# Attention and gated feed-forward on one core: the ordering's TensorE durations set to the trace, and 90 idle products for 160

## The chip, the core and the metric

The kernel runs on one core of a Trainium2 chip. TensorE multiplies matrices, VectorE (DVE), ScalarE (ACT) and GpSimd (POOL) work on elements, SyncE (SP) issues the DMAs. The metric is the device time of one execution in microseconds; the time of a kernel is the median of its runs. A profiled execution has its own time, and the span from its first to its last instruction lies inside it.

## The reference

```python
# q, k, v: (4, 8, 768, 64) f32; n_sink = 4, window = 128
scores = q @ k.T / 8
keep = (pos_k < n_sink) | ((0 <= rel) & (rel < window))     # rel = pos_q - pos_k
a = softmax(where(keep, scores, -1e9)); attn = a @ v
x = attn.transpose(0, 2, 1, 3).reshape(3072, 512)
h = x @ w_in                       # (512, 2048), float64
out = (h * cos(h)) @ w_out         # (2048, 512), float64, result f32
```

Only a band of 128 keys and the first few (the sinks) are kept for each query, and everything behind it is a feed-forward layer whose two products are most of the work.

## The kernel before

**Tiling.** The 3072 tokens are 12 chunks of 256 (two blocks of 128 queries). A chunk has 8 heads of attention and then 8 *slots* of the feed-forward layer; a slot is 256 of the 2048 inner columns. Products are made in fp32r with each operand split into a high and a low part, so each is three matmuls: high by high, high by low, low by high.

**A head.** The scores `s` (line 739 for the first 24 heads, "early" ones, in plain fp32; line 795 for the others) go into one PSUM tile with one buffer. The mask step (808, VectorE) adds the mask and takes the row's extreme; the next score needs that tile back. Then come the exponential (817, ScalarE), the denominator (826, 827, VectorE), the normalisation (835 on ScalarE or 837 on VectorE or POOL), the transposition `tp` (897, TensorE), a copy or a split of it (368, 370, 906, 913), the product with V, `av` (927 early, 951 later), and the split of the result into `xhi` and `xlo`. An early head makes the low part with a small matmul against minus the identity (325). Early heads also turn q and k on TensorE (715, `qk`).

**A slot.** `h` (379) is 24 matmuls in four steps of six. Then: turns (388, ScalarE), whole and rest (394, 399, VectorE), cosine (404, ScalarE), gate (409, VectorE), the split into `ghi` (415, ScalarE) and `glo` (421, VectorE or POOL), and `acc` (430), 12 matmuls in four steps of three. After the eighth slot the two output blocks are copied (368 or 370) and stored.

**Weights.** They come as float64 in 32 pieces through two raw buffers. VectorE turns each into f32 in three steps (483, 489, 495), ScalarE rounds it to the high part (516), VectorE or POOL makes the low part (519). Later all pieces are read again for a range check (534). This conversion runs beside the attention of the first chunks.

**What sets the order.** Nothing is left to run-time choice but waiting: each engine has one fixed list. `Plan.order` makes the lists at build time. Every step has the engines that could do it, an expected duration on each, its predecessors, the buffers it needs and a due time. The planner walks forward in expected time; when an engine is free it takes the ready step with the earliest due time, and where several engines could do a step, the expected durations decide who takes it. A change of ScalarE's table between exponential and cosine is charged. The expected durations thus set the order on all engines, though no instruction depends on them. `GATE` is when the engines are expected to begin, `PRE` when VectorE and ScalarE may begin the steps marked `ahead` (the weight steps); what starts before `GATE` is written ahead of the program's branch. `SPE` is the expected delay from any other engine's step to TensorE.

**Idle products.** `fill` (line 1174 of the profile) is a 128x128 by 128x256 matmul of the minus identity into a PSUM tile nobody reads. `FILL` of them are given to the planner with due times behind everything else, so TensorE takes one whenever no other step is ready in the planner's time, until they are used up.

Of the kernel before, what the change touches and what calls it, by code (L numbers as in the profile page):

```python
# [28 lines left out]
    "DV": 4.41, "DX": 7.018, "FILL": 160, "GHI": 2, "GLO": 2, "L": 1, "LAG": 4.21, "LEAD": 18.263, "NEH": 24,  # L29
    "NM": 1.373, "NW": 2.093, "NWF": 0.026, "PB": 5, "PEN": 10.744, "PL": 3, "POOLF": 0.675, "POOLPEN": 2.303,  # L30
    "PRE": 4.5, "R": 2, "RAW": 2, "SAME": 0.13, "SEM": 0.2, "SPE": 0.3, "STEP": 5.59, "T": 6.142, "TH": -1.227,
    "WARM": 11, "WI": -18.566, "WO": 7.302, "WS": 1.56, "WS2": -0.177, "WT": 2, "XV": 2,
}
GATE = 5.4
# [138 lines left out]
def attn_moe_kernel(ctx, tc, q, k, v, n_sink, window, w_in, w_out, out):  # L173
# [20 lines left out]
    NEH = int(C["NEH"]) // 2 * 2  # L194
# [106 lines left out]
    env = Rec()  # L301
# [38 lines left out]
    def split_x(plan, x, a, p, t, odd=None):  # L340

        add, buf = plan.add, plan.buf
# [7 lines left out]
        if odd is None:  # L350
            j = add(sub(NT), x_lo(x, a, p, odd), d, t + 0.3, port=True)
        else:
            m = add([("PE", 0.11)], x_minus(x, p, odd), [i], t + 0.3)
            users.append(m)
            env.minus.users.append(m)
            j = add([("ACT", act(NT, False)), ("DVE", dve(NT))], x_lo(x, a, p, odd), d + [m], t + 0.6)
# [188 lines left out]
    def dense(plan, x, a, s, t, T, w_in_ready, w_out_ready, acc_banks, h_bank):  # L545
# [8 lines left out]
        if True:  # L554
# [23 lines left out]
            for tt in range(FG):  # L578
                for j in range(CB):
                    d = [a5, a6] + w_out_ready[s] + (accs[j].users[:1] or [accs[j]])  # L580
                    late = 2.6 * j if a == len(chunks) - 1 and s >= NSLOT - 2 else 0.3 * j
                    i = add([("PE", 0.655)], out_mm(o, x, tt, j), d, t + C["LAG"] * T + (0.0, 1.95)[tt] + late)
# [21 lines left out]
    def banded_path():  # L604
# [383 lines left out]
        def before_softmax(g, o):  # L988
# [111 lines left out]
        def after_softmax(g, o):  # L1100
# [4 lines left out]
            if o.early:  # L1105
# [44 lines left out]
            y0 = add([("PE", 0.5)], values(o), deps, t + C["DA"] + 4.0)  # L1150
# [28 lines left out]
        for n in range(int(C["FILL"])):  # L1179
            idle.users.append(add([("PE", 0.11)], fill(n), idle.users[:1] or [idle, env.minus], 1e4 + n))  # L1180
# [229 lines left out]
```

## Time and profile before

| what | value |
|---|---|
| time, median of 3 runs | 789.77 us (788.59 to 789.86) |
| profiled execution | 790.24 us |
| its span | 788.4 us, granted TensorE clock 0.994 |
| TensorE busy | 762.5 us, 97% |
| VectorE, ScalarE, POOL busy | 641.8, 577.5, 172.0 us |
| HBM read | 64.10 MB |

A line of the groups reads: line, engine, operation, output <- inputs, shapes, count, then busy time and the mean of one in ns, then the engine's idle time before these instructions and what ended it. A matmul's record includes its way through the array, so matmuls overlap; what one costs in a sequence is read from start to start. A line of the timeline begins with start and duration in us. A line of waits reads: who <- for whom, us in total, times, longest.

### The profile page before, as it was taken

The page shows a single profiled execution, that of the slowest core. Times are in us where ns is not written, and L with a number is a line of the kernel's source. Part 1 is how long each engine was busy: PE and PEld are TensorE (multiplying, and loading weights), DVE is VectorE, ACT ScalarE, POOL GpSimd, SP SyncE. Part 2 cuts the span into 40 slices and gives each one's busy share as a digit, 9 for nine tenths or more (in the row PEclk, how much of TensorE's full clock was granted, in tenths as well). Part 3 has the DMA queues.
Part 4 walks back from the last instruction along what each step waited for, and adds up shares of the span by engine and source line. Part 5 has one row for each costly group of instructions (what it writes and reads, how often), then busy time and mean ns, then how long its engine had stood idle before and what let it go on. Part 6 is the DMA issues. An engine that isn't in the chain of part 4 may idle for free.

```text
span 788.4 us, 15691 instructions
## 1 busy us (share of the span) xinstructions
PE 762.5 (97%) x5087; PEld 671.9 (85%) x5087; DVE 641.8 (81%) x1672; ACT 577.5 (73%) x1363; POOL 172.0 (22%) x239
## 2 busy tenths in 40 slices
PE   7999999999999999999999999999999999999996
PEld 6766777788999889898989899999998999999994
DVE  5777889876899879879979999889789979875442
ACT  1666878688787787787887877888898887785332
POOL 1113111000112214232233334322012232420000
PEclk8999999999999999999999999999999999999999
DMA  5554455423275265346455442332142242210000
GB/s 149 152 155 116 140 155 154 110 62 56 42 181 123 47 167 145 79 121 160 104 134 153 109 103 49 55 75 42 34 86 53 47 87 38 42 38 6 27 1 32
DMA packets 215676, 71.53 MB, mean 91 GB/s; under 512 B 204320, under 2 KB 204320, under 8 KB 215584
## 3 DMA queue, kind: packets, MB, share of 16 engines
q1 hardware_dynamic: 215584, 70.43, 37.6%
q8 instruction: 42, 0.69, 0.4%
q14 instruction: 50, 0.41, 0.2%
HBM read 64.10 MB, written 6.29 MB: 89 GB/s over the span
## 4 chain that ended last, share of the span: by engine, by line
PE 73%; DVE 13%; DMA 6%; ACT 3%; SPq 2%; issue 2%; DVEq 0%; POOL 0%; ACTq 0%; POOLq 0%
PE h L379 26%; PE acc L430 25%; PE tp L897 4%; PE av L951 4%; PE s L795 4%; DMA raw<-in_moe_w_out_dram 3%; PE idle L1174 3%; PE s L739 3%; PE av L927 2%; DMA raw<-in_moe_w_in_dram 2%; DVE p L808 1%; SPq L677 1%; DVE wt L534 1%; DVE r L399 1%; DMA xq<-in_q_dram 1%
## 5 line engine op out<-in xcount | busy, mean ns | idle before, releaser
L379 PE MATMUL h<-xhi,whi_in 128*128 128x256 f32 x768 | 224.4, 292 | 2.6 <-DVE r L409 2.6
L379 PE MATMUL h<-xlo,whi_in 128*128 128x256 f32 x768 | 216.4, 282 | 0.0
L379 PE MATMUL h<-xhi,wlo_in 128*128 128x256 f32 x768 | 216.3, 282 | 0.0
L379 PEld LDWEIGHTS h<-xhi,whi_in 128*128 128x128 f32 x768 | 145.2, 189 | 16.3 <-issue 5.2
L430 PE MATMUL acc<-whi_out,ghi 128*128 128x512 f32 x384 | 155.6, 405 | 0.0
L430 PE MATMUL acc<-wlo_out,ghi 128*128 128x512 f32 x384 | 151.4, 394 | 0.0
L379 PEld LDWEIGHTS h<-xhi,wlo_in 128*128 128x128 f32 x768 | 145.5, 189 | 6.8
L430 PE MATMUL acc<-whi_out,glo 128*128 128x512 f32 x384 | 150.6, 392 | 0.0
L379 PEld LDWEIGHTS h<-xlo,whi_in 128*128 128x128 f32 x768 | 145.2, 189 | 0.1
L808 DVE CUSTOM_DVE_ANT_0 p<-s,mk 128x264 f32<-128x264 f32 (+1 forms) x192 | 76.4, 398 | 24.9 <-PE s L795 12.1
L817 ACT ACTIVATE p<-p,st 128x264 f32<-128x264 f32 (+1 forms) x192 | 93.2, 488 | 0.5
L430 PEld LDWEIGHTS acc<-whi_out,glo 128*128 128x128 f32 x384 | 72.2, 188 | 16.6
L404 ACT ACTIVATE r<-r 128x512 f32<-128x512 f32 x96 | 59.7, 631 | 35.6 <-DVE r L399 32.2
L850 POOL TENSOR_TENSOR vr<-v,vr 128x192 fp32r<-128x192 f32 (+1 forms) x63 | 41.1, 652 | 172.4 <-ACT vr L845 127.1
L415 ACT CAST ghi<-r 128x512 fp32r<-128x512 f32 x96 | 59.0, 615 | 24.8 <-PE acc L430 23.0
L430 PEld LDWEIGHTS acc<-whi_out,ghi 128*128 128x128 f32 x384 | 72.5, 189 | 5.1 <-issue 0.5
L430 PEld LDWEIGHTS acc<-wlo_out,ghi 128*128 128x128 f32 x384 | 72.9, 190 | 4.3
L409 DVE TENSOR_TENSOR r<-h,r 128x512 f32<-128x512 f32 x96 | 64.4, 679 | 13.1 <-ACT r L404 12.7
L399 DVE TENSOR_TENSOR r<-yt,r 128x512 f32<-128x512 f32 x96 | 74.0, 770 | 1.0
L421 DVE TENSOR_TENSOR glo<-r,ghi 128x512 fp32r<-128x512 f32 x71 | 49.6, 699 | 29.3 <-ACT ghi L415 28.8
L795 PE MATMUL s<-r,l 128*128 128x264 f32 (+2 forms) x288 | 62.7, 295 | 6.8 <-DVE r L786 3.8
L388 ACT ACTIVATE yt<-h 128x512 f32<-128x512 f32 x96 | 57.0, 593 | 8.3 <-PE h L379 6.5
(128 smaller groups left out, 1471.2 us busy)
## 6 DMA issues: line engine op xcount, KB each, us to landing
raw<-in_moe_w_in_dram SPq DMA_DIRECT2D x32, 512.0 KB, 4.6
raw<-in_moe_w_out_dram SPq DMA_DIRECT2D x32, 512.0 KB, 3.7
xk<-in_k_dram SPq DMA_DIRECT2D x256, 48.0 KB, 2.0
out_dram<-raw SPq DMA_DIRECT2D x24, 256.0 KB, 2.2
v<-in_v_dram SPq DMA_DIRECT2D x64, 96.0 KB, 2.1
xq<-in_q_dram SPq DMA_DIRECT2D x144, 32.0 KB, 1.9
v<-in_v_dram SPq DMA_DIRECT2D x32, 64.0 KB, 2.0
xq<-in_q_dram SPq DMA_DIRECT2D x24, 64.0 KB, 2.5
```

Source lines behind the costliest of these rows:

```text
L379: nc.tensor.matmul(out=o.h[:, t, :], lhsT=w[:, c, fs], rhs=xx[:, c, :], start=(c == 0 and n == 0), stop=(c == NC - 1 and n == 2),)
L388: nc.scalar.activation(out=o.y, in_=o.h, func=AF.Copy, scale=INV2PI, bias=0.25)
L399: e.tensor_tensor(out=o.r, in0=o.y, in1=o.r, op=ALU.subtract)
L404: nc.scalar.activation(out=o.r, in_=o.r, func=AF.Sin, scale=TWOPI_DOWN)
L409: nc.vector.tensor_tensor(out=o.r, in0=o.h, in1=o.r, op=ALU.mult)
L415: nc.scalar.copy(out=o.ghi, in_=o.r)
L421: e.tensor_tensor(out=o.glo, in0=o.r, in1=f32(o.ghi), op=ALU.subtract)
L430: nc.tensor.matmul(out=x.acc[j], lhsT=gg[:, t, j * P : (j + 1) * P], rhs=w[:, f, :], start=(f == 0 and n == 0), stop=(f == NFT - 1 and n = ...
L795: nc.tensor.matmul(out=o.s_ps[j][:, :w], lhsT=o.l[:, j * P : (j + 1) * P], rhs=r.rearrange("p n s -> p (n s)")[:, c0 : c0 + w], start=(n = ...
L808: nc.vector.tensor_tensor_reduce(out=o.p[:, j, :w], in0=o.s_ps[j][:, :w], in1=masks[min(o.i0 + j, 2)][:, :w], op0=ALU.add, op1=ALU.min, sc ...
L817: nc.scalar.activation(out=o.p[:, j, :w], in_=o.p[:, j, :w], func=AF.Exp, bias=o.lead.st[:, 0, o.nth, j : j + 1], scale=-1.0, accum_out=o. ...
L850: e.tensor_tensor(out=o.vr[:, :, 1, :], in0=o.v32, in1=f32(o.vr)[:, :, 0, :], op=ALU.subtract)
```

## The change

The expected durations of TensorE's steps are replaced: a step of `h` 0.714 us instead of 0.655, of `acc` 0.696 instead of 0.655, an early score `w / 650 + 0.235` instead of `w / 600 + 0.02`, other scores 0.245 instead of 0.23, an early `av` 0.15 longer, a later one 0.64 instead of 0.5 where the sinks are in it, the small matmul of line 325 0.3 instead of 0.11, an idle product 0.12 instead of 0.11. `GATE` goes from 5.4 to 9.0, `PRE` from 4.5 to 7.3, `SPE` from 0.3 to 0.2. `FILL` goes from 160 to 90. The arithmetic of the result is untouched; the lists of all five engines come out in another order.

```diff
-    "DV": 4.41, "DX": 7.018, "FILL": 160, "GHI": 2, "GLO": 2, "L": 1, "LAG": 4.21, "LEAD": 18.263, "NEH": 24,
+    "DV": 4.41, "DX": 7.018, "FILL": 90, "GHI": 2, "GLO": 2, "L": 1, "LAG": 4.21, "LEAD": 18.263, "NEH": 24,
-    "PRE": 4.5, "R": 2, "RAW": 2, "SAME": 0.13, "SEM": 0.2, "SPE": 0.3, "STEP": 5.59, "T": 6.142, "TH": -1.227,
+    "PRE": 7.3, "R": 2, "RAW": 2, "SAME": 0.13, "SEM": 0.2, "SPE": 0.2, "STEP": 5.59, "T": 6.142, "TH": -1.227,
-GATE = 5.4
+GATE = 9.0
...
-                        add([("PE", 0.655)], h_mm(o, x, tt, half), d + mm[-1:], t + C["DH"] + (3.5, 5.8)[tt] + 0.6 * half)
+                        add([("PE", 0.714)], h_mm(o, x, tt, half), d + mm[-1:], t + C["DH"] + (3.5, 5.8)[tt] + 0.6 * half)
...
-                    i = add([("PE", 0.655)], out_mm(o, x, tt, j), d, t + C["LAG"] * T + (0.0, 1.95)[tt] + late)
+                    i = add([("PE", 0.696)], out_mm(o, x, tt, j), d, t + C["LAG"] * T + (0.0, 1.95)[tt] + late)
...
-                    dur, fn, deps, used = o.w[j] / 600 + 0.02, scores_pe(o, oe, j), oe.kr, (oe.btq, oe.btk)
+                    dur, fn, deps, used = o.w[j] / 650 + 0.235, scores_pe(o, oe, j), oe.kr, (oe.btq, oe.btk)
...
-            idle.users.append(add([("PE", 0.11)], fill(n), idle.users[:1] or [idle, env.minus], 1e4 + n))
+            idle.users.append(add([("PE", 0.12)], fill(n), idle.users[:1] or [idle, env.minus], 1e4 + n))
```

More of the change, by code (lines that the diff above doesn't have):

```diff
@@ L352, in split_x @@
         else:
-            m = add([("PE", 0.11)], x_minus(x, p, odd), [i], t + 0.3)
+            m = add([("PE", 0.3)], x_minus(x, p, odd), [i], t + 0.3)
             users.append(m)
@@ L1064, in before_softmax @@
                     oe = heads[g - o.odd]
-                    dur, fn, deps, used = o.w[j] / 600 + 0.02, scores_pe(o, oe, j), oe.kr, (oe.btq, oe.btk)
+                    dur, fn, deps, used = o.w[j] / 650 + 0.235, scores_pe(o, oe, j), oe.kr, (oe.btq, oe.btk)
                 else:
-                    dur, fn, deps, used = 0.23, scores(o, j), [o.ql, *o.kr], (o.bl, b1, b2)
+                    dur, fn, deps, used = 0.245, scores(o, j), [o.ql, *o.kr], (o.bl, b1, b2)
                 c0 = add([("PE", dur)], fn, [*deps, bs], t - 5 * T + C["DS"] + (3.25, 5.55)[j])
@@ L1115, in after_softmax @@
                 y0 = add(
-                    [("PE", 0.215 * o.n + 0.05)], values_pe(o, x), [p1, i, x.y0 if o.odd else x.bav], t + C["DA"] + 4.0
+                    [("PE", 0.215 * o.n + 0.2)], values_pe(o, x), [p1, i, x.y0 if o.odd else x.bav], t + C["DA"] + 4.0
                 )
@@ L1149, in after_softmax @@
                 deps += oe.sinks
-            y0 = add([("PE", 0.5)], values(o), deps, t + C["DA"] + 4.0)
+            y0 = add([("PE", 0.64 if o.sj else 0.5)], values(o), deps, t + C["DA"] + 4.0)
             for bb in (bvr, bhi, blo):
```

## The prediction

> **What bounds the kernel now.** I read the engine shares first, then the chain of work that ended last, then TensorE's own row of time by stage.
>
> ```profile
> span 788.4 us, 15691 instructions
> PE 762.5 (97%) x5087; PEld 671.9 (85%) x5087; DVE 641.8 (81%) x1672; ACT 577.5 (73%) x1363; POOL 172.0 (22%) x239
> ...
> by line: PE h L379 26.4%; PE acc L430 24.8%; PE tp L897 4.1%; PE av L951 4.1%; PE s L795 3.6%; DMA raw<-in_moe_w_out_dram 3.1%; PE idle L1174 2.9%; PE s L739 2.6%; issue 2.4%; PE av L927 2.2%; DMA raw<-in_moe_w_in_dram 2.1%; DVE p L808 1.1%
> ```
>
> TensorE sets the time: 97% busy, and the chain runs mostly through it. The entry to look at is `PE idle L1174`: 2.9% of 788.4 is 22.9 us in which the chain passes through products that nobody needs. Where they stand is told by the stretches (PE busy, PEld, DVE, ACT, POOL, granted clock, DMA share, GB/s):
>
> ```profile
> 10.00:20.00 10.00, 10.00 (x55) 8.38 (x53) 7.83 (x25) 1.98 (x4) 0.00 (x0) 0.77 0.53 147
> 20.00:30.00 10.00, 9.88 (x65) 8.01 (x64) 7.68 (x24) 6.85 (x24) 0.73 (x1) 1.00 0.49 137
> ...
> 50.00:60.00 10.00, 9.95 (x57) 6.79 (x56) 7.64 (x21) 5.54 (x14) 2.74 (x3) 1.00 0.63 171
> ...
> 200.00:300.00 100.00, 97.28 (x686) 88.53 (x685) 88.52 (x240) 78.66 (x188) 24.09 (x35) 1.00 0.50 115
> 300.00:400.00 100.00, 97.20 (x689) 88.80 (x687) 91.03 (x245) 78.52 (x192) 32.79 (x44) 1.00 0.49 116
> ...
> L1174 PE MATMUL idle<-gt x160: 274/283/580, 9.9 to 70.9; 128*128 128x256 f32 x160
> ...
> DVE p L808 <- PE s L739: 8.0, 15, 1.3
> ```
>
> All 160 idle products start between 9.9 and 70.9 us, and there TensorE is full. The last row is VectorE's waits between 8 and 75 us: it waited 8.0 us for scores. In that stage the others wait for TensorE, not TensorE for them, so the idle products cost time instead of filling it.
>
> **The change part by part.** First the 70 products that go. Three prices from the trace:
>
> ```profile
> 25.28 1.58 PE L1174 MATMUL idle<-gt 128*128 128x256 f32 x11
> 26.79 0.70 PE L739 MATMUL s<-tk,tq 64*128 64x256 f32 x2
> ...
> 69.81 0.64 PE L1174 MATMUL idle<-gt 128*128 128x256 f32 x4
> 70.29 0.49 PE L897 MATMUL tp<-ident,p 128*128 128x128 f32 x3
> ```
>
> Start to start, 11 of them take 26.79 - 25.28 = 1.51 us, 0.137 each; 4 take 0.48 us, 0.12 each; the chain says 22.9 / 160 = 0.143. So 70 are worth 8.4 to 10.0 us. I take 0.13 and **-9.0 us**, if what stands behind them is ready.
>
> That it is not always ready is the second part. On TensorE, from a transposition of the probabilities (tp) to the product that uses it (av), head 6 of the first chunk; before:
>
> ```order
> L897 MATMUL tp_0_6_659<-ident,p_0_6_508 128x128 x3
> L325 MATMUL av_0_4_619<-xhi_426,gt 64x256
> L1174 MATMUL idle<-gt 128x256 x6
> L715 MATMUL qk_0_4_680<-ident,xq 128x128 x2
> L1174 MATMUL idle<-gt 128x256
> L739 MATMUL s_0_2_0_686<-tk_0_2_668,tq_0_2_664 128x128
> L715 MATMUL qk_0_4_680<-ident,xk 128x128 x2
> L897 MATMUL tp_0_7_694<-ident,p_0_7_556 128x128 x3
> L927 MATMUL av_0_6_698<-pt_0_6_672,v_0_76 64x256
> ```
>
> and in the changed order:
>
> ```order
> L897 MATMUL tp_0_6_620<-ident,p_0_6_482 128x128 x3
> L739 MATMUL s_0_1_1_624<-tk_0_0_548,tq_0_0_543 128x256
> L1174 MATMUL idle<-gt 128x256
> L927 MATMUL av_0_6_631<-pt_0_6_626,v_0_76 64x256
> L927 MATMUL av_0_6_631<-pt_0_6_626,v_0_76 64x128
> L897 MATMUL tp_0_7_641<-ident,p_0_7_521 128x128 x3
> ```
>
> Seven rows lay between head 6's tp and its av; now one score and one idle product do. What the copy between them needs, and what a score needs until its mask is done:
>
> ```profile
> 28.11 0.49 PE L897 MATMUL tp<-ident,p 128*128 128x128 f32 x3
> 28.64 0.56 DVE L370 COPY pt<-tp 128x384 f32<-128x384 f32 x1 [0.68 <-PE tp L897]
> ...
> 19.33 0.70 PE L739 MATMUL s<-tk,tq 64*128 64x256 f32 x2
> 19.95 1.46 PE L1174 MATMUL idle<-gt 128*128 128x256 f32 x10
> 20.06 0.42 DVE L808 CUSTOM_DVE_ANT_0 p<-s,mk 128x256 f32<-128x256 f32 x1 [1.26 <-PE s L739]
> 20.41 0.08 DVE L808 DVE_READ_ACCUMULATOR2_ANT st<- 128x1 f32 x1
> 20.41 0.69 DVE L489 SCALAR_TENSOR_TENSOR wt<-raw,wt 128x512 int32<-128x512 int32 x1
> ...
> 28.45 0.50 ACT L817 ACTIVATE p<-p,st 128x256 f32<-128x256 f32 x1
> ```
>
> From the transposition's start to the copy's end 28.64 + 0.56 - 28.11 = 1.09 us. The new order gives it about 0.3 (three transpositions) + 0.62 (the score, 19.95 - 19.33) + 0.12 = 1.04 us: just enough when the copying engine is free, too little when an exponential (0.50) is ahead on ScalarE. Adding up the rows in this way, 6 of the 24 early heads had under 1.5 us of products between tp and av; now 18 have. Twelve more heads at 0 to 0.50 us: 0 to 6 us; I take 0.2 each, **+2.4**, since a copy is taken by whichever of two engines is free. Scores share one PSUM tile, so the next must wait for the mask before: 20.49 - 19.33 = 1.16 us after the score's start, of which 0.62 are its own, so 0.54 of other work has to follow. Of the early scores, one had under 1.0 us of it, now 13 have, and one only 0.31. At 0 (the mask comes at once) to 0.69 (a weight step is ahead of it): 0 to 8 us; I take under 0.1 each, **+1.0**, as the weight steps also stand elsewhere now.
>
> Third, VectorE's start. GATE and PRE put two weight steps (L489) before the branch and the sink parts of V (L857, L858) ahead of the first mask. VectorE now, from the masks' constants on:
>
> ```order
> L495 SCALAR_TENSOR_TENSOR wt_73<-raw_71,wt_73 128x512
> L1228 COPY mk<-mk 128x8
> L1229 TENSOR_TENSOR mk<-mk 128x128
> L857 CAST vs<-xb 16x4x64
> L1230 TENSOR_TENSOR mk<-mk 128x128
> L1231 COPY mk<-mk 128x128
> L858 TENSOR_TENSOR vs<-xb,vs 16x4x64
> L1232 TENSOR_SCALAR mk<-mk 128x648
> L857 CAST vs<-xb 16x4x64
> L858 TENSOR_TENSOR vs<-xb,vs 16x4x64
> L808 ISA p_0_0_233,st_0_0_234<-s_0_0_0_215,mk 128x128
> ```
>
> Before, the four vs steps came after the second mask:
>
> ```profile
> 13.45 0.49 DVE L1232 TENSOR_SCALAR mk<-mk 128x648 f32<-128x648 f32 x1
> 14.10 0.29 DVE L808 CUSTOM_DVE_ANT_0 p<-s,mk 128x128 f32<-128x128 f32 x1
> ...
> 16.30 0.42 DVE L808 CUSTOM_DVE_ANT_0 p<-s,mk 128x256 f32<-128x256 f32 x1 [0.69 <-PE s L739]
> 16.64 0.28 DVE L857 CAST vs<-xb 16x256 fp32r<-16x256 f32 x1
> ...
> 17.72 0.41 DVE L858 TENSOR_TENSOR vs<-xb,vs 16x256 fp32r<-16x256 f32 x1
> ```
>
> They run from 16.64 to 18.13, 1.5 us, which now delay the first mask; but VectorE stood idle 0.69 us before the second, and is relieved of the 1.5 us right after. 0 to 1.5 us late; I take **+0.5**. The loads change places on SyncE's queue (two raw weights before the second key tile), and the raw buffers are freed at the same L495 as before: 0.
>
> Fourth, the remaining 700 us. With slower TensorE steps expected, VectorE is given more: 13 more glo (L421), 17 more normalisations net (L837), 6 more output copies; ScalarE gets 18 more table loads. For one batch, normalisations that stood on POOL
>
> ```order
> L837 TENSOR_SCALAR p_2_0_5281<-p_2_0_5281,st_2_0_5282 128x264 x2
> L837 TENSOR_SCALAR p_2_1_5410<-p_2_1_5410,st_2_0_5282 128x264
> L837 TENSOR_SCALAR p_2_2_5511<-p_2_2_5511,st_2_0_5282 128x264 x2
> L837 TENSOR_SCALAR p_2_3_5628<-p_2_3_5628,st_2_0_5282 128x264
> L850 TENSOR_TENSOR vr_2_1_5877<-v_1_77,vr_2_1_5877 128x3x64
> ```
>
> stand on VectorE, ahead of the next gate (L409) and mask:
>
> ```order
> L827 RECIPROCAL st_2_0_5132<-st_2_0_5132 128x8
> L837 TENSOR_SCALAR p_2_0_5131<-p_2_0_5131,st_2_0_5132 128x264 x2
> L837 TENSOR_SCALAR p_2_1_5291<-p_2_1_5291,st_2_0_5132 128x264 x2
> L837 TENSOR_SCALAR p_2_2_5434<-p_2_2_5434,st_2_0_5132 128x264
> L867 CAST gc<-p_2_0_5131 128x2x8
> ```
>
> ```profile
> L421 DVE TENSOR_TENSOR glo<-r,ghi 128x512 fp32r<-128x512 f32 x71 | 49.6, 699 | 29.3 <-ACT ghi L415 28.8 <-issue 0.2
> L837 DVE TENSOR_SCALAR p<-p,st 128x264 f32<-128x264 f32 x39 | 15.6, 455 | 0.3
> L370 DVE COPY raw<-acc 128x512 f32<-128x512 f32 x11 | 7.6, 690 | 3.5 <-PE acc L430 3.4
> L404 ACT ACT_TABLE_LOAD x29 | 37.2, 1283 | 1.7 <-DVE st L826 1.3
> L958 ACT COPY xb<-av 64x256 f32<-64x256 f32 x72 | 26.6, 369 | 42.2 <-PE av L951 41.0
> ...
> 377.72 2.06 PE acc L430 x9
> ...
> 456.58 1.42 PE h L379 x12
> ...
> PE s L795 <- DVE r L786: 3.8, 4, 1.7
> PE s L795 <- DVE st L808: 1.7, 2, 1.5
> ```
>
> VectorE: 13 x 0.699 + 17 x 0.455 + 6 x 0.690 = 21 us more, 641.8 to 663; ScalarE: 18 x 1.283 = 23 us. What covers ScalarE's is its own 41 us of waiting for av, and the products between a slot's last h and its first acc: at 1.42 us for 12 h and 2.06 for 9 acc (the two pieces of the chain), the rows there add up to 20 us or more for nine slots in ten up to the last chunk, before and now. What covers VectorE's is the 9 to 11.5 us per 100 that it stands idle at 200 to 400 us (over the whole span 28.8 us go to waiting for ghi). The last two rows are TensorE's main waits at 250 to 475 us, 7.0 us in all, every one for VectorE. An order that fits TensorE's real pace could save half of them, -3; a fifth of the added work on the path would cost +4. Nothing decides between them: **0**.
>
> Sum: -9.0 + 2.4 + 1.0 + 0.5 + 0 = **-5.1 us** against the profiled execution of 790.24 us (span 788.4 and 1.84 around it): 785.1. That execution lies 0.47 above the median of 789.77, so the median should fall to **784.7**. The change does remove the 70 products, by the order itself, so that it does nothing is no rival.
>
> **The rivals.** *All of it is kept*: -9 stays, and the mid waits shrink by 3; about 778. For it: TensorE is busy 9.9 to 10.0 of 10 in the early rows, so it hardly ever waited there. Against: the thin places above. *Nothing arrives*: the next bound, VectorE at 7.6 of 10 in the early rows and loading weights beside the masks, takes over as soon as TensorE runs ahead, and gives the 9 us back; 789.8. Against: 2.4 of 10 are free there. *Slower, by VectorE's added work*: between 200 and 400 us it is busy 88.5 and 91 of 100, and the moved work stands ahead of masks and of r (L786), for which TensorE waits. If 40% of the 21 us lands on TensorE, +8.4 against -5.1: 793; it is slower from a quarter on. Against it: the work went to places where the idle time was. *The clock*: it stood at 0.77 at 10 to 20 us, after a gap of 4.1 us (first row below). If thinner products let it fall once more, the 2.3 us lost there and 1.1 (0.89) before come again: 788.1.
>
> ```profile
> 1.36 4.12 PE L245 MATMUL warm<-ident 128*128 128x128 f32 x22 [1.36 <-POOL ident L233]
> 9.58 0.66 PE L715 MATMUL qk<-ident,xq 128*128 128x128 f32 x2 [4.10 <-DMA xq<-in_q_dram]
> 0.00:10.00 10.00, 4.54 (x25) 4.38 (x25) 2.94 (x19) 1.28 (x1) 2.77 (x12) 0.89 0.53 146
> ```
>
> The Trainium skill (TensorE: Matmul & The Clock Gate, on the HAM clock gate) says that the clock halves after an idle window of about 3.4 us. The 4.1 us gap and the 0.77 behind it agree; by that rule the 90 products that stay, with no gap of that length between them, keep the clock at 1.00.
>
> **How the numbers follow.** Forecast 0.48 (own range 781.5 to 787.5), all kept 0.16, nothing arrives 0.13, slower 0.20, clock 0.03. A measurement here can tell about 0.2%, 1.6 us, from no change. Faster: 0.48 + 0.16 + 0.03 = 0.67; same 0.13; slower 0.20. The range runs from the best sum (-10.0 - 3 = 776.8) to the slower case: 777 to 793.
>
> **What would show it.** `idle L1174` x90, 9 us less of it on the chain. New TensorE waits before 75 us, for pt (L368/L370) and for masks (L808): 3 to 4 us where there were next to none. First h about 5 us before 48.51, where it starts now:
>
> ```profile
> 48.51 0.29 PE L379 MATMUL h<-xhi,whi_in 128*128 128x256 f32 x1
> ```
>
>  VectorE near 663 busy. Waits at 250 to 475 us within 3 us of 7.0. Wrong, if TensorE waits over 9 us more in either stage, or if the gain at first h is gone by 200 us.

## The result, and the profile after

The changed kernel takes 816.79 us (median of 4 runs, 809.19 to 818.23) against 789.82 for the kernel before beside it: a ratio of 1.0319, 95% interval 1.025 to 1.0387. The forecast was 784.7, the range 777 to 793. It is 27 us slower where 5 us were to be gained.

The page of the changed kernel, profiled at 815.92 us: the span, the busy times, and the chain of work that ended last, by engine and by line.

```profile
span 813.8 us, 15550 instructions
PE 773.9 (95%) x5017; PEld 668.4 (82%) x5017; DVE 661.4 (81%) x1732; ACT 596.6 (73%) x1369; POOL 137.3 (17%) x191
...
PE 45%; DVE 23%; ACT 13%; DMA 10%; issue 6%; SPq 2%; DVEq 0%; POOL 0%; ACTq 0%; POOLq 0%
PE h L379 15%; PE acc L430 14%; ACT p L817 3%; DMA raw<-in_moe_w_out_dram 3%; DMA raw<-in_moe_w_in_dram 3%; PE s L739 3%; PE tp L897 3%; DVE p L837 2%; PE av L951 2%; PE s L795 2%; ACT L817 2%; PE av L927 2%; DVE r L399 2%; DVE p L808 2%; DVE plo L913 2%
```

The same line of the page before:

```profile
PE 73%; DVE 13%; DMA 6%; ACT 3%; SPq 2%; issue 2%; DVEq 0%; POOL 0%; ACTq 0%; POOLq 0%
```

TensorE still looks full (95%), but only 45% of the chain runs through it, against 73%. VectorE is busy 661.4 us, as forecast (663). ScalarE went from 3% of the chain to 13%; `ACT L817` is the loading of a table ahead of the exponential.

Stretches of the changed kernel (PE busy, PEld, DVE, ACT, POOL, granted clock, DMA share, GB/s; the number behind x is the count of instructions):

```profile
60.00:70.00 10.00, 8.17 (x45) 5.61 (x43) 9.25 (x28) 9.43 (x29) 0.62 (x1) 0.93 0.53 165
70.00:80.00 10.00, 10.00 (x34) 6.31 (x33) 7.10 (x16) 6.35 (x14) 4.06 (x3) 0.56 0.41 106
200.00:300.00 100.00, 95.27 (x656) 85.17 (x654) 88.38 (x238) 80.94 (x182) 16.71 (x24) 1.00 0.51 116
300.00:400.00 100.00, 93.60 (x647) 83.24 (x646) 89.88 (x242) 75.46 (x183) 26.74 (x40) 1.00 0.48 113
400.00:500.00 100.00, 93.77 (x647) 83.31 (x647) 89.50 (x245) 78.80 (x181) 24.27 (x29) 1.00 0.46 106
500.00:600.00 100.00, 97.48 (x664) 87.46 (x663) 83.63 (x230) 82.77 (x190) 12.94 (x22) 1.00 0.27 50
600.00:700.00 100.00, 97.33 (x658) 86.61 (x656) 85.70 (x229) 84.65 (x188) 18.61 (x27) 1.00 0.29 57
```

and those stretches of the kernel before that the prediction did not show:

```profile
70.00:80.00 10.00, 8.72 (x50) 5.74 (x50) 8.39 (x22) 5.46 (x11) 3.01 (x3) 1.00 0.28 81
...
400.00:500.00 100.00, 97.99 (x688) 88.84 (x687) 90.00 (x237) 80.18 (x193) 32.30 (x47) 1.00 0.48 111
500.00:600.00 100.00, 100.00 (x710) 92.58 (x710) 87.41 (x240) 84.76 (x204) 23.59 (x32) 1.00 0.29 55
600.00:700.00 100.00, 99.95 (x706) 91.63 (x706) 87.94 (x234) 81.62 (x191) 30.39 (x40) 1.00 0.29 57
```

Read the counts, not the busy time. From 500 to 600 us TensorE is busy 97.48 instead of 100.00, which looks like 2.5 us, but it begins 664 matmuls instead of 710, 6.5% fewer, at a granted clock of 1.00 in both. A matmul's record is longer than its turn in the sequence (a mean of 282 ns for most matmuls of h, of which the next starts 0.12 us later in a dense row), so a short stall hides behind the record before it. The other loss is seen in the second row: from 70 to 80 us the clock is at 0.56 and 34 matmuls begin where 50 did.

To see when time is lost I weighed every matmul except the idle products by the usual start-to-start time of its kind in the kernel before (its 10th percentile; 661.7 us in all), and compared when the same sum of work was reached (good to some 0.3 us). Lateness against the kernel before, in us, at that kernel's times (negative is ahead); the numbered kernels are the experiments below:

| kernel | 60 | 100 | 200 | 300 | 400 | 500 | 600 | 700 | 780 |
|---|---|---|---|---|---|---|---|---|---|
| changed kernel | -3.2 | -0.8 | -2.6 | 0.4 | 6.8 | 12.8 | 20.7 | 25.3 | 25.4 |
| the same, 160 idle products (e2) | -4.3 | -2.6 | 0.5 | 1.8 | 5.6 | 9.2 | 16.7 | 21.1 | 21.3 |
| before, 90 idle products (e1) | 6.4 | 9.8 | 10.3 | 9.5 | 8.9 | 7.8 | 7.8 | 7.9 | 7.9 |
| before, h and acc longer (e3) | -0.4 | -0.6 | 0.0 | 1.6 | 1.7 | 2.3 | 5.6 | 9.6 | 9.6 |
| small steps alone (e13) | -5.6 | -2.4 | -1.6 | -2.5 | -3.1 | -1.3 | -1.0 | -0.5 | -0.5 |
| small steps, 110 idle products (e20) | -4.5 | -2.9 | -4.1 | -5.4 | -6.1 | -5.7 | -5.3 | -4.8 | -4.8 |

The changed kernel is ahead at the start, by less than was forecast. It loses 28 us between 200 and 700 us, most of it where the prediction had put zero.

### The profile page after: what moved, and what is told of

The parts are those of the page before. It is cut to its first block, busy times and chain, and to the rows that moved or that the text cites. A ratio compares the mean times of both kernels' runs of the same rounds, so it can differ in the third digit from the quotient of the medians.

```text
span 813.8 us, 15550 instructions
## 1 busy us (share of the span) xinstructions
PE 773.9 (95%) x5017; PEld 668.4 (82%) x5017; DVE 661.4 (81%) x1732; ACT 596.6 (73%) x1369; POOL 137.3 (17%) x191
## 4 chain that ended last, share of the span: by engine, by line
PE 45%; DVE 23%; ACT 13%; DMA 10%; issue 6%; SPq 2%; DVEq 0%; POOL 0%; ACTq 0%; POOLq 0%
PE h L379 15%; PE acc L430 14%; ACT p L817 3%; DMA raw<-in_moe_w_out_dram 3%; DMA raw<-in_moe_w_in_dram 3%; PE s L739 3%; PE tp L897 3%; DVE p L837 2%; PE av L951 2%; PE s L795 2%; ACT L817 2%; PE av L927 2%; DVE r L399 2%; DVE p L808 2%; DVE plo L913 2%
## 5 line engine op out<-in xcount | busy, mean ns | idle before, releaser
L817 ACT ACTIVATE p<-p,st 128x264 f32<-128x264 f32 (+1 forms) x192 | 93.4, 490 | 0.6
L421 DVE TENSOR_TENSOR glo<-r,ghi 128x512 fp32r<-128x512 f32 x84 | 59.7, 711 | 32.4 <-ACT ghi L415 32.1
L430 PEld LDWEIGHTS acc<-whi_out,glo 128*128 128x128 f32 x384 | 72.1, 188 | 16.5
L795 PE MATMUL s<-r,l 128*128 128x264 f32 (+2 forms) x288 | 66.0, 302 | 7.4 <-DVE r L786 2.9
L399 DVE TENSOR_TENSOR r<-yt,r 128x512 f32<-128x512 f32 x96 | 67.4, 703 | 1.0
L850 POOL TENSOR_TENSOR vr<-v,vr 128x192 fp32r<-128x192 f32 (+1 forms) x55 | 34.9, 634 | 196.7 <-ACT vr L845 157.6
```

The source lines that it names most:

```text
L399: e.tensor_tensor(out=o.r, in0=o.y, in1=o.r, op=ALU.subtract)
L421: e.tensor_tensor(out=o.glo, in0=o.r, in1=f32(o.ghi), op=ALU.subtract)
L430: nc.tensor.matmul(out=x.acc[j], lhsT=gg[:, t, j * P : (j + 1) * P], rhs=w[:, f, :], start=(f == 0 and n == 0), stop=(f == NFT - 1 and n = ...
L795: nc.tensor.matmul(out=o.s_ps[j][:, :w], lhsT=o.l[:, j * P : (j + 1) * P], rhs=r.rearrange("p n s -> p (n s)")[:, c0 : c0 + w], start=(n = ...
L817: nc.scalar.activation(out=o.p[:, j, :w], in_=o.p[:, j, :w], func=AF.Exp, bias=o.lead.st[:, 0, o.nth, j : j + 1], scale=-1.0, accum_out=o. ...
L850: e.tensor_tensor(out=o.vr[:, :, 1, :], in0=o.v32, in1=f32(o.vr)[:, :, 0, :], op=ALU.subtract)
```

## The experiments

Each experiment had runs of the kernel before beside it (medians 788.6 to 790.3); ratios are against those. The planner's count of ScalarE's table changes in an order is named where it matters: 69 for the kernel before, 87 for the changed kernel (the traces have 58 and 76 table loads, the same 18 more).

### Idle products and the clock

**e1_fill90**: the kernel before, only with fewer idle products.

```diff
-    ... "FILL": 160, ...
+    ... "FILL": 90, ...
```

> The kernel before with FILL 90 for 160 and nothing else. Three theories. 'Margin': the short TensorE durations made the planner take TensorE for idle part of the time, so that every other engine stood ahead of it in reality; with true durations each step is placed just when its inputs are expected, and whatever comes later than expected stalls TensorE. 'Any other order': the due-time constants were fitted to this one order and any reshuffle costs 10 to 30 us. 'Idle products': these 70 themselves matter (clock, early stage). Margin: 70 x 0.13 = 9 us less, 781. Any other order: 795 to 815. Idle products: slower than before, 795 or more.

Measured: 798.31 us (790.47 to 803.23), ratio 1.009 [1.0056, 1.0125]. Taking out the 70 products alone was to bring 9 us; it costs 0.9%, 7 us by the ratio and 9 by the medians. Its stretches:

```profile
30.00:40.00 10.00, 8.57 (x40) 4.94 (x37) 8.52 (x27) 6.73 (x22) 1.26 (x1) 0.92 0.63 173
40.00:50.00 10.00, 10.00 (x31) 5.94 (x31) 6.55 (x17) 5.46 (x18) 0.00 (x0) 0.50 0.39 122
...
70.00:80.00 10.00, 10.00 (x42) 8.45 (x42) 5.06 (x15) 6.58 (x23) 1.35 (x1) 0.53 0.22 66
80.00:90.00 10.00, 8.70 (x52) 5.91 (x50) 6.25 (x18) 6.58 (x14) 1.54 (x2) 1.00 0.44 133
```

The granted clock is at half for some 40 us, with TensorE "busy" throughout. Across its ten executions the mean granted clock and the time go together: 0.981 and 0.982 with 790.5 to 791.9 us, 0.964 to 0.971 with 797.8 to 803.2. So the idle products do something: in this order they hold the clock.

**e16_fill130**: the same edit with 130.

```diff
-    ... "FILL": 160, ...
+    ... "FILL": 130, ...
```

> The kernel before with 130 idle products in place of 160. If 130 still hold the clock until the first h products, the 30 that go are worth 0.13 us each: 785 to 787 us. If the clock falls as in e1_fill90 (half from 38 to 79 us there, 798.31 us), 793 to 798 us and a granted clock under 0.985.

Measured: 787.86 us (783.80 to 792.38), ratio 0.9976 [0.9951, 1.0001]. The clock fell here too, to 0.66 in the profile's 70 to 80 us, but only for some 10 us; the ratio stands for 1.9 of the 3.9 us that 30 products are worth, at the edge of the noise.

**e18_steps_fill90**: the changed kernel with h and acc back at 0.655 and GATE and PRE as before, so that the durations of tp, s and av, SPE, and the 90 idle products stay. It is e13_steps_old_gate (below) with 90 for 160.

Against the changed kernel:

```diff
-    "PRE": 7.3, ...
+    "PRE": 4.5, ...
-GATE = 9.0
+GATE = 5.4
...
-                        add([("PE", 0.714)], h_mm(o, x, tt, half), d + mm[-1:], t + C["DH"] + (3.5, 5.8)[tt] + 0.6 * half)
+                        add([("PE", 0.655)], h_mm(o, x, tt, half), d + mm[-1:], t + C["DH"] + (3.5, 5.8)[tt] + 0.6 * half)
...
-                    i = add([("PE", 0.696)], out_mm(o, x, tt, j), d, t + C["LAG"] * T + (0.0, 1.95)[tt] + late)
+                    i = add([("PE", 0.655)], out_mm(o, x, tt, j), d, t + C["LAG"] * T + (0.0, 1.95)[tt] + late)
```

> e13_steps_old_gate (790.23 us, 160 idle products) with 90 idle products: h and acc at 0.655, gate 5.4 and PRE 4.5 as before, tp, s and av at the durations of the change. In e1_fill90 the 90 products alone cost 8 us, since the clock was at half from 38 to 79 us; in the changed kernel, whose first h products come at 42 us, the clock fell later, from 69 to 79 us. If the earlier h products (43 us in e13_steps_old_gate) hold the clock in place of the idle ones: 781 to 786 us. If it falls as in e1_fill90: 796 to 802 us, granted clock 0.965 to 0.982.

Measured: 787.23 us; seven executions took 785.25 to 789.88 and three, at a granted clock of 0.961 to 0.966, 799.45 to 803.62. The ratio of the seven is 0.9977 [0.9957, 0.9997]. Its first h starts at 40.4 us and the clock still fell, later. First its stretches, then rows of its timeline (start and duration in us, and in brackets the idle time ahead), then, of the kernel before, the row behind its gap at 72 us:

```profile
60.00:70.00 10.00, 7.67 (x44) 5.37 (x42) 9.39 (x26) 8.80 (x22) 1.57 (x2) 0.95 0.48 140
70.00:80.00 10.00, 10.00 (x34) 6.69 (x34) 5.00 (x15) 5.09 (x10) 2.47 (x2) 0.50 0.23 65
80.00:90.00 10.00, 10.00 (x56) 7.66 (x56) 7.71 (x19) 6.83 (x23) 0.00 (x0) 0.87 0.50 140
```
```profile
64.60 0.86 PE L927 MATMUL av<-pt,v 128*64 128x256 f32 x4 [0.57 <-ACT pt L368]
...
67.81 0.33 PE L325 MATMUL av<-xhi,gt 64*64 64x256 f32 x1 [1.24 <-ACT xhi L317]
```
```profile
72.41 0.70 PE L739 MATMUL s<-tk,tq 64*128 64x256 f32 x2 [1.27 <-DVE st L808]
```

Gaps of 0.57 and 1.24 us, some 3 us apart, stand ahead of the fall at 69 us. Behind a single one of 1.27, with a dense row of h and idle products ahead of it, the clock stayed (1.00 from 70 to 80 us in the kernel before). Even this execution, one of the seven, had the clock at half for some 13.6 us in all.

**e20_steps_fill110**: e18 with 110; the order of all other rows is the same.

```diff
-    ... "FILL": 90, ...
+    ... "FILL": 110, ...
```

> e18_steps_fill90 (787.23 us, three of its ten executions at a granted clock of 0.961 to 0.966 and 799 to 804 us) with 110 idle products: the order of everything else is the same, row by row. If 20 more products hold the clock, 20 x 0.13 = 2.6 us more than the undisturbed executions of e18_steps_fill90 (785.2 to 787.7): 787 to 790 us, and no execution under 0.975. If the clock falls in some executions all the same, some of 798 us and more will be among them.

Measured: 784.24 us (781.52 to 786.67), ratio 0.9926 [0.9898, 0.9955], and no execution under a clock of 0.985. This beats both kernels, and the 787 to 790 us that were expected from e18's seven, which were not free of the half clock. Its stretch where e18 fell, and one earlier:

```profile
70.00:80.00 10.00, 8.03 (x47) 5.34 (x44) 8.58 (x19) 5.63 (x14) 2.65 (x2) 1.00 0.31 101
30.00:40.00 10.00, 9.04 (x35) 6.17 (x35) 7.83 (x25) 5.16 (x17) 2.59 (x4) 0.66 0.54 151
```

Against e13 (ratio 1.0019, 160 products) 50 products fewer bring 0.0093 x 789 = 7.3 us, 0.147 each (0.08 to 0.21 by the two intervals): the price in the prediction (0.12 to 0.143) was right where the clock is alike. It is alike here, and not unbroken: both profiles have 0.66 from 30 to 40 us, 6.8 us at half. Twenty fewer still (e18) bring nothing more.

### Which durations cost

**e2_fill160**: the changed kernel with 160 idle products again.

```diff
-    ... "FILL": 90, ...
+    ... "FILL": 160, ...
```

> The changed kernel with 160 idle products again. Margin: the loss stays and the 70 products come on top, 816.8 + 9 = 826. Any other order: 800 to 830, no sign foretold. Idle products: back near 790 to 800.

Measured: 811.53 us (810.53 to 814.54), ratio 1.0295 [1.0265, 1.0325], at a granted clock of 0.994 to 0.996. With the clock held, 2.95% of the 3.19% stay: the order is the main loss.

**e4_nudge**: the kernel before with h at 0.657, which moves 1768 of TensorE's 4498 rows.

```diff
-                        add([("PE", 0.655)], h_mm(o, x, tt, half), d + mm[-1:], t + C["DH"] + (3.5, 5.8)[tt] + 0.6 * half)
+                        add([("PE", 0.657)], h_mm(o, x, tt, half), d + mm[-1:], t + C["DH"] + (3.5, 5.8)[tt] + 0.6 * half)
```

> The kernel before with the step of h at 0.657 for 0.655, a 0.3% change that means nothing but moves 1768 of 4498 TensorE rows to another place. Margin: no change beyond 5 us, 785 to 795. Any other order: 800 to 815.

Measured: 788.56 us, ratio 0.9993 [0.9977, 1.001]. So another order need not cost anything.

**e3_dense**: h 0.714 and acc 0.696, nothing else.

```diff
-                        add([("PE", 0.655)], h_mm(o, x, tt, half), d + mm[-1:], t + C["DH"] + (3.5, 5.8)[tt] + 0.6 * half)
+                        add([("PE", 0.714)], h_mm(o, x, tt, half), d + mm[-1:], t + C["DH"] + (3.5, 5.8)[tt] + 0.6 * half)
...
-                    i = add([("PE", 0.655)], out_mm(o, x, tt, j), d, t + C["LAG"] * T + (0.0, 1.95)[tt] + late)
+                    i = add([("PE", 0.696)], out_mm(o, x, tt, j), d, t + C["LAG"] * T + (0.0, 1.95)[tt] + late)
```

> The kernel before with only the two dense durations changed: a step of h 0.714 for 0.655, of acc 0.696 for 0.655. They are 541 us of TensorE's work and 96 slots go by them. Margin: most of the loss by itself, 27 us + 9 us that the idle products gave back, so 815 to 825 with 160 idle products; waits of tp, gp, s and av at 250 to 700 us as in the changed kernel. Any other order: 800 to 830. If the start (GATE, PRE) or the attention steps' durations are the cause: 785 to 795.

Measured: 799.98 us (799.11 to 802.89), ratio 1.0151 [1.0123, 1.0179]: half of the loss of e2.

**e9_all_but_dense**: e2 with h and acc back at 0.655.

```diff
-                        add([("PE", 0.714)], h_mm(...
+                        add([("PE", 0.655)], h_mm(...
-                    i = add([("PE", 0.696)], out_mm(...
+                    i = add([("PE", 0.655)], out_mm(...
```

> The changed kernel with 160 idle products (e2_fill160, 811.53 us) with h and acc back at 0.655: every other edit of the order stays (tp 0.3, s 0.235 and 0.245, av, gate 9.0, PRE 7.3, SPE 0.2). ScalarE's table changes are 69 in its order, as before; 85 in e2_fill160. Theory W: no added change of table, so 787 to 792 us. Theory M: the small steps of TensorE are still at their true durations, and these made up the half of the loss that e3_dense did not show: 797 to 803 us.

Measured: 796.49 us (794.41 to 799.57), ratio 1.0079 [1.0046, 1.0112].

**e13_steps_old_gate**: e9 with GATE 5.4 and PRE 4.5.

```diff
-    "PRE": 7.3, ...
+    "PRE": 4.5, ...
-GATE = 9.0
+GATE = 5.4
```

> e9_all_but_dense (796.49 us) with the gate at 5.4 and PRE at 4.5 again, as before: what stays of the change are the durations of tp, s and av, the y0 and idle durations, and SPE 0.2. In e9_all_but_dense the 192nd h product started at 130.4 us, 7.4 us later than in the kernel before, and the stretch from there to the 2304th took 643.2 us, against 646.5 before. If the gate and PRE are what makes the start longer there: 192nd h at 122 to 124 us, 785 to 789 us. If the steps' durations make it: 192nd h at 129 to 131 us, 794 to 797 us. Theory X: the middle is no more than luck, 793 to 800 us.

Measured: 790.23 us (787.79 to 797.13), ratio 1.0019 [0.9989, 1.005]. So GATE and PRE cost 0.6%, 4.7 us, and the durations of tp, s and av nothing. The place was not the expected one: the 192nd h started at 128.5 us, hardly earlier than in e9 (130.4); by the sum of work e9 is 2.4 us behind e13 at 60 us and 4.6 at the end.

### Why longer h and acc cost

The first theory was ScalarE's added table changes (W) against a plan too tight for TensorE (M). PEN is the planner's penalty for a table change.

**e7_dense_pen14**: e3_dense with PEN 14; 57 table changes against its 81.

```diff
-    ... "PEN": 10.744, ...
+    ... "PEN": 14, ...
```

> The kernel before with the longer durations for h (0.714) and acc (0.696) alone, as in the run called e3_dense (799.98 us), and with the planner's penalty for a change of ScalarE's table (PEN) at 14 in place of 10.744. In its order ScalarE changes its table 57 times; it does so 69 times in the kernel before and 81 times in e3_dense. Theory W (what the reordering costs is ScalarE's added table changes, some 0.9 us each on the chain that sets the end: 11 us for 12 in e3_dense): 12 fewer than before, 778 to 790 us. Theory M (with the true durations of TensorE the planner puts each step of the other engines just in time, and whatever is late on the chip stalls TensorE, however many changes of table there are): 797 to 803 us, as e3_dense.

Measured: 794.24 us (792.43 to 801.16), ratio 1.007 [1.004, 1.0099].

**e8_pen4**: the kernel before with PEN 4; 95 table changes.

```diff
-    ... "PEN": 10.744, ...
+    ... "PEN": 4, ...
```

> The kernel before with nothing but PEN at 4 in place of 10.744: TensorE's durations as before, ScalarE's table changes go from 69 to 95 in the order. Theory W: 26 more at 0.9 us each, about 813 us (805 to 820). Theory M: the durations that the planner holds for TensorE are as before, so 788 to 792 us.

Measured: 797.44 us (796.49 to 802.64), ratio 1.0102 [1.0074, 1.013].

**e14_pen14**: the kernel before with PEN 14; 57 table changes.

```diff
-    ... "PEN": 10.744, ...
+    ... "PEN": 14, ...
```

> The kernel before with nothing but PEN at 14 in place of 10.744: 57 table changes in the order, against 69, with TensorE's durations as before. If a table change costs 0.26 us on the path, the slope between e8_pen4 and before and between e3_dense and e7_dense_pen14: 12 fewer are 3 us, 786 to 788 us. Theory X: 793 to 800 us, since 3007 of 4498 rows of TensorE stand at another place.

Measured: 790.40 us (786.89 to 794.27), ratio 1.0009 [0.998, 1.0038].

Both theories fell as they were put. Twenty-six more changes cost 1.0%, 24 fewer bring 0.8% back in e3's order, but 12 fewer bring nothing in the order before. It may be that table changes cost only where ScalarE is on the path already; PEN moves other rows too, so this is not shown.

**e11_others**: TensorE as before, the planner's durations of VectorE, ScalarE and GpSimd x 0.926.

```diff
-    SWITCH = 1.28
+    SWITCH = 1.18
...
-        return ((n / 2 if two else n) + 62) / 960 + (0.06 if ptr else 0)
+        return 0.926 * (((n / 2 if two else n) + 62) / 960 + (0.06 if ptr else 0))
...
```

> The kernel before with TensorE's durations untouched, and those that the planner holds for VectorE, ScalarE and GpSimd lowered by 0.926 (its price of a table change from 1.28 to 1.18). TensorE then stands to the other engines in the plan as it does in e3_dense (799.98 us), though no duration of TensorE has moved. Table changes in the order: 75, against 69 before. Theory B (what counts is the proportion of the durations that the planner holds: TensorE's alone were raised, so the plan believes that the other engines have more room than they have): 797 to 805 us. Theory M (TensorE's own durations decide, because with the true ones its steps are placed just in time): 788 to 792 us, 1 to 2 us of it for 6 added table changes at 0.26 us, the slope that e8_pen4 and e7_dense_pen14 gave.

Measured: 794.33 us (793.24 to 796.08), ratio 1.0059 [1.0037, 1.0081], between the two theories. By the sum of work it is 1.9 us ahead at 500 us and 5.8 behind at 700: no duration of TensorE has moved, and still it loses 7.7 us where e3_dense loses 7.3. Its stretches there:

```profile
500.00:600.00 100.00, 98.71 (x686) 89.45 (x685) 88.67 (x245) 81.37 (x189) 15.76 (x26) 1.00 0.29 56
600.00:700.00 100.00, 98.43 (x677) 88.02 (x676) 84.51 (x228) 85.74 (x194) 17.04 (x24) 1.00 0.25 48
```

**e10_scaled**: e3_dense with the others' durations x 1.08.

```diff
-    SWITCH = 1.28
+    SWITCH = 1.38
...
-        return n / 1200 + (0.092 if sbuf else 0.051)
+        return 1.08 * (n / 1200 + (0.092 if sbuf else 0.051))
...
```

> e3_dense (h 0.714, acc 0.696) with the durations that the planner holds for VectorE, ScalarE and GpSimd raised by 1.08 as well, and its price of a table change from 1.28 to 1.38, so that TensorE stands to the other engines as it did in the kernel before. Table changes in the order: 69, as before. Theories W and M agree here: 788 to 793 us. If it is as slow as e3_dense (797 to 803), neither holds, and it is the longer plan against fixed due times that costs.

Measured: 799.18 us (797.46 to 800.84), ratio 1.0102 [1.0049, 1.0155]: the proportion restored, the time not. But the loss is another one. By the sum of work e10 is 2.0 us ahead at 200 us, 10.7 behind at 500 and 10.4 at the end, so it loses nothing from 500 on, and more than half of what it loses before is clock. Two rows of the timeline and the stretch behind them:

```profile
421.69 0.28 PE L795 MATMUL s<-r,l 128*128 128x264 f32 x1
424.84 0.39 PE L795 MATMUL s<-r,l 128*128 128x264 f32 x1 [2.87 <-DVE r L786]
```
```profile
420.00:430.00 10.00, 7.13 (x36) 6.05 (x36) 6.83 (x22) 5.74 (x14) 2.80 (x6) 0.83 0.72 172
```

One stall of 2.87 us, and for about 3.4 us after it the clock is at half (10 us x 0.17 x 2), 1.7 us more. Four such falls, each 0.83 in its 10 us, stand between 230 and 430 us: 6.8 us. From 500 us on its matmuls are as many as in the kernel before:

```profile
500.00:600.00 100.00, 99.99 (x704) 91.98 (x703) 87.36 (x235) 82.99 (x203) 20.25 (x31) 1.00 0.30 58
600.00:700.00 100.00, 100.00 (x708) 92.38 (x707) 86.59 (x236) 83.30 (x190) 25.81 (x38) 1.00 0.28 52
```

The third reading named ahead of this run, a longer plan against fixed due times, is neither shown nor excluded: no run moves the due times along.

**e12_dense60**: h and acc at 0.60, the change's direction turned round.

```diff
-                        add([("PE", 0.655)], h_mm(...
+                        add([("PE", 0.60)], h_mm(...
-                    i = add([("PE", 0.655)], out_mm(...
+                    i = add([("PE", 0.60)], out_mm(...
```

> The kernel before with h and acc at 0.60 in place of 0.655, the change's direction turned round. Table changes: 63. Theory M (shorter durations give each step more room on the chip): 784 to 789 us. Theory B (the proportion is what counts): with TensorE too short the plan holds the other engines back behind it for longer, no loss of room for them: 786 to 792 us. Theory X (the order before is a good one among many, and whatever moves as many rows of TensorE as 3600 of 4498 costs some us, in either direction): 793 to 800 us.

Measured: 800.32 us (796.67 to 802.32), ratio 1.0135 [1.0096, 1.0173]. Shorter costs as much as longer; M and the proportion theory B, as they were put, both fail here. Theory X, by which any order far from the one before costs some us, fits this run but not e13 and e14, for which it had foretold 793 to 800 us.

**e17_dense683**: half way up.

```diff
-                        add([("PE", 0.655)], h_mm(...
+                        add([("PE", 0.683)], h_mm(...
-                    i = add([("PE", 0.655)], out_mm(...
+                    i = add([("PE", 0.683)], out_mm(...
```

> The kernel before with h and acc at 0.683, half way to the trace's durations; 0.714 and 0.696 gave 799.98 us, 0.60 gave 800.32, 0.657 gave 788.56. Table changes in the order: 75. Theory V (a valley around the proportion of 0.655: the farther from it on either side, the more work of other engines falls late): 793 to 796 us. Theory X (each order is a draw, and the distance from 0.655 says nothing): anywhere from 789 to 801 us; outside 791 to 797 it speaks against V.

Measured: 794.59 us (793.20 to 797.85), ratio 1.0072 [1.0045, 1.0099], as a valley would have it. With e4, e12 and e3 the ratios over the duration of h are 1.0135 (0.60), 1 (0.655), 0.9993 (0.657), 1.0072 (0.683), 1.0151 (0.714).

**e19_dense_pool**: e3_dense with GpSimd favoured (POOLF 0.6).

```diff
-    ... "POOLF": 0.675, ...
+    ... "POOLF": 0.6, ...
```

> e3_dense (h 0.714, acc 0.696; 799.98 us) with the planner's factor for GpSimd's durations (POOLF) at 0.6 in place of 0.675: in the order GpSimd does 158 of the normalisations and glo copies that VectorE could do as well, against 70 in e3_dense and 86 in the kernel before. Theory G (the kernels with longer h and acc lose their time from 500 to 700 us, where GpSimd worked 54 us in the kernel before, 41 in e3_dense, 32 in e2_fill160: work moved from GpSimd to VectorE makes the attention steps late): 787 to 793 us. If the share of GpSimd only goes along with the loss and does not make it: 797 to 803 us. If GpSimd's slower instructions become the wait themselves: over 803 us.

Measured: 803.06 us (800.68 to 805.05), ratio 1.017 [1.0137, 1.0203]. VectorE fell to 622.7 us busy, below the 641.8 of the kernel before, and nothing was gained. How much VectorE has to do in all is not the cause. (Some 3 us of this run's stalls from 200 to 700 us are waits for GpSimd's own normalisations, so part of a gain could hide there; most of its stalls after 500 us, 4.4 of 6.1 us, still end with VectorE.) Stretches of e3_dense, and then of e19_dense_pool:

```profile
500.00:600.00 100.00, 99.08 (x682) 89.24 (x681) 86.46 (x237) 83.92 (x192) 21.75 (x31) 1.00 0.28 55
600.00:700.00 100.00, 98.18 (x677) 88.08 (x678) 85.76 (x230) 84.02 (x189) 19.69 (x27) 1.00 0.27 50
```
```profile
500.00:600.00 100.00, 97.91 (x673) 88.31 (x671) 76.86 (x204) 84.28 (x197) 32.54 (x53) 1.00 0.29 56
600.00:700.00 100.00, 99.29 (x684) 89.45 (x685) 84.02 (x223) 83.67 (x193) 27.50 (x44) 1.00 0.27 50
```

VectorE has 10 us more to spare in the first hundred, and TensorE begins 673 matmuls instead of 682 there and 684 instead of 677 in the second.

**e15_repaired**: all of the change's TensorE durations, but GATE, PRE and FILL as before and PEN 14.

```diff
-    ... "FILL": 90, ... "PEN": 10.744, ... "PRE": 7.3, ...
+    ... "FILL": 160, ... "PEN": 14, ... "PRE": 4.5, ...
-GATE = 9.0
+GATE = 5.4
```

> The changed kernel with every duration that it gives TensorE's steps kept (h 0.714, acc 0.696, tp, s, av), but with gate 5.4, PRE 4.5 and 160 idle products as before and PEN at 14. If the parts add up as they did one by one (gate and PRE +6, idle products 5 to 9, the table changes that longer h and acc bring some 6 of their 10), what is left is what e7_dense_pen14 showed, +4: 792 to 797 us. If the small steps' true durations, harmless in e13_steps_old_gate, cost once h and acc are longer too: 800 to 806 us.

Measured: 803.00 us (799.58 to 811.27), ratio 1.016 [1.0126, 1.0195]. The parts do not add up: the small steps' durations, free in e13, cost 0.9% more than e7 once h and acc are longer too.

**Where the stalls are.** The start-to-start times of TensorE from 500 to 700 us, split into the usual time of each kind (as above) and what goes beyond it, in us:

| kernel | usual | over by less than 150 ns | by 150 to 1500 ns | by more |
|---|---|---|---|---|
| before | 183.4 | 16.5 | 0.2 | 0 |
| e13 | 182.4 | 16.4 | 1.1 | 0 |
| e3 | 176.4 | 17.4 | 6.1 | 0 |
| e19 | 176.9 | 17.0 | 6.1 | 0 |
| e2 | 172.8 | 17.4 | 9.8 | 0 |
| changed | 172.8 | 17.0 | 10.2 | 0 |
| e7 | 178.8 | 16.8 | 4.4 | 0 |
| e8 | 182.1 | 16.4 | 1.5 | 0 |
| e11 | 176.0 | 18.2 | 5.9 | 0 |
| e10 | 184.1 | 15.8 | 0.2 | 0 |
| e12 | 180.3 | 15.3 | 2.6 | 1.5 |

In e2, of the stalls over 150 ns 6.0 us stand ahead of scores (795), 1.7 ahead of gp (879), 1.1 ahead of av (951) and 0.9 ahead of tp (897); by the trace 9.1 of them end with a step of VectorE. In the kernel before all these steps together stall for 0.2 us after 500 us. So the loss of this stage is located and sized: attention steps that come up on TensorE a little before VectorE has done with their inputs, many times.

For this stage the runs also tell what makes them late, by one order of each kind. e3 raises the planned durations of TensorE alone: 6.1 us. e11 lowers those of the other engines alone: 5.9. e10 raises all of them alike: 0.2, as in the kernel before. So it is the proportion, theory B, and not TensorE's durations as such (M): the plan counts on the other engines being faster beside TensorE than they are. The share of GpSimd does not make it (e19). Nor do table changes alone: 24 fewer take off 1.7 of the 6.1 us (e7), and e8, with the most of all, has 1.5. What makes the 8.7 us that e2 loses between 200 and 500 us, and the loss of e12 with the opposite proportion, stays open.

## Why the prediction was wrong, by its own steps

**First, -9.0 for 70 products.** The price held, within its noise: 0.147 each in e20 against e13. The condition ("if what stands behind them is ready") named the wrong danger. What was left out of account is the clock: TensorE's row from 10 to 70 us was full *because of* these products, and from 30 us on at 1.00 for the same reason (0.92 and then 0.50 in e1). In the order before, -9 became +7 to +9 (e1). In the changed order, whose clock was at half from 69 to 79 us, going back to 160 gains 2 us by the ratios (1.0319 and 1.0295), within their intervals, and 5 by the medians: there -9 became +2 to +5.

**The clock rival** was given 0.03 and 2.3 + 1.1 us. Its mechanism was right and its size was off by a factor of three to five: from -9 to +2 or +5 are 11 to 14 us in the changed order, and to some +8 are 17 in the order before. The prediction priced a fall by the gap before it, and took over the rule of the Trainium skill (TensorE: Matmul & The Clock Gate, on the HAM clock gate) that it takes an idle window of about 3.4 us. By that rule the 90 products would have kept 1.00. The rows say otherwise: the clock fell after gaps of 1.24 and 0.57 us in e18, and after 2.87 in e10. The length of the falls in e10, 3.4 us each, does agree with the window that the Trainium skill gives there. In the early stage the clock stayed down for some 10 us (changed kernel), 13.6 (e18) and 41 (e1, where it came back at 79 us, 9 us after the first h).

**Second, +2.4 and +1.0.** Waits of TensorE from 8 to 75 us, changed kernel and then before:

```profile
PE s L739 <- DVE st L808: 2.7, 3, 1.5
PE tp L897 <- ACT p L835: 1.1, 1, 1.1
PE av L325 <- ACT xlo L368: 0.7, 1, 0.7
```
```profile
PE s L739 <- DVE st L808: 1.3, 1, 1.3
PE av L325 <- ACT xlo L368: 0.2, 1, 0.2
```

4.5 us against 1.5, 3.0 more, as forecast (3 to 4). But not for the copies of pt: for masks, for a normalisation and for a split.

**Third, +0.5 for GATE and PRE.** Right in sign, mis-sized: 4.7 us (e9 against e13).

**Fourth, "the remaining 700 us: 0".** This is the step that failed. Its bounds were -3 and +4; it is some 20 us (21.3 us of lateness at the end of e2, against 0.5 at 200 us), 12 of them behind 500 us. VectorE's added work came as counted, and so did ScalarE's table loads. Groups of the changed kernel, and one of the kernel before:

```profile
L421 DVE TENSOR_TENSOR glo<-r,ghi 128x512 fp32r<-128x512 f32 x84 | 59.7, 711 | 32.4 <-ACT ghi L415 32.1
L404 ACT ACT_TABLE_LOAD x38 | 48.8, 1283 | 4.8 <-DVE r L399 3.0 <-DVE st L826 1.2
L817 ACT ACT_TABLE_LOAD x37 | 47.5, 1283 | 0.6
```
```profile
L817 ACT ACT_TABLE_LOAD x28 | 35.9, 1283 | 0.5
```

What failed is the cover. The prediction laid the added work against idle time summed over a stage (41 us of ScalarE's waits, 28.8 of VectorE's). Idle time is cover only where the late step has slack, and many attention steps had none: VectorE went from 13% to 23% of the chain, ScalarE from 3% to 13%. The prediction asked how much work moved; from 500 us on what counted is the proportion of the planned durations, which the change shifted by raising TensorE's alone (e3, e11, e10). The waits listed from 250 to 475 us, changed kernel, longest first:

```profile
PE s L795 <- DVE r L786: 2.1, 2, 1.8
PE tp L897 <- DVE plo L913: 1.9, 2, 1.7
PE tp L897 <- DVE p L837: 1.8, 1, 1.8
PE h L379 <- DVE xlo L335: 1.7, 2, 1.1
PE gp L879 <- DVE gc L869: 1.6, 3, 1.0
PE tp L897 <- ACT p L835: 1.6, 1, 1.6
PE av L951 <- DVE plo L913: 1.5, 2, 0.8
```

With the smaller ones 14.5 us, against 7.0 forecast to stay within 3. That is 7.5 us more, under the 9 named as the mark of being wrong, though more than 9 us of lateness arose there: the list of waits is short of the stalls (in e2 it has 4.1 us from 500 to 700 us, the start-to-start times 9.8). The other mark, the lead gone by 200 us, came late: 2.6 us were left at 200, none at 300.

**The slower rival** (793, by VectorE's added work landing on TensorE) had the right sign and place, at 8.4 us for 40% of 21. Its reason, the sum of VectorE's work, is not borne out: with VectorE relieved (e19) the loss stays. But the waits after 500 us are for VectorE, as it said.

**What was right**: the 90 products, the first h earlier than 48.51 (by 6.4 us, forecast about 5), VectorE's busy time, and the early waits.

```profile
42.06 0.39 PE L379 MATMUL h<-xhi,whi_in 128*128 128x256 f32 x1
```

## What to carry to other kernels

Before useless-looking matmuls are taken out, look at what the granted clock does in the stretch that they fill, and take them out in steps: 50 of 160 brought 7.3 us, 20 more nothing, and in the order before, 70 cost 7 to 9 us. A number that only sets an order is not made better by being made true: h and acc cost 1.4 to 1.5% on either side of their value in the kernel before, and with longer h and acc the stalls after 500 us went only when the other engines' numbers were raised in proportion (e10). An order is judged by the chip alone. Where work is moved, ask for the slack of the step that becomes late, not for the idle time of the engine, and read TensorE's progress from its counts of matmuls.

## What the runs showed of the hardware

The granted clock fell to half without any long gap: in e1_fill90 at about 38.4 us, where in the 4 us before TensorE was busy 3.24 us by the profile, with transpositions, scores of 64 rows and other small products, and had one idle stretch of 0.71 us (a second one, of 0.66, began as the clock fell). It fell behind two gaps of 1.24 and 0.57 us in e18, and not behind one of 1.27 in the kernel before, with a dense row ahead of it. What decides is not the gap alone: in e13_steps_old_gate, with 160 idle products, it fell at about 33 us, 2.5 us after a single gap of 1.05 us. Once down, it stayed down for 3.4 us (e10), 6.8 (e13, e20), 10 (changed kernel), 13.6 (e18) or 41 (e1). The same program differs from execution to execution in this: e1 took 790.5 to 803.2 us, e18 785.2 to 803.6, with the mean granted clock at 0.98 or at 0.96, while 110 idle products in e18's order gave 781.5 to 786.7. And a stall of 2.87 us in the middle (e10) cost a further 1.7 us by the half clock behind it.
